# Shorter score bursts, 512-wide first products and a ScalarE-first order in a planned attention and two-MLP kernel

## The chip, the cores and the metric

The kernel runs on one core of a Trainium2 chip. The metric is device time in microseconds of one execution; the median of several executions is compared. Engines are named as the profile names them: PE is TensorE (PEld its weight loads), DVE VectorE, ACT ScalarE, POOL GpSimd, SP SyncE, which here issues nearly all DMAs.

## What is computed

```python
# attention, B=2, S=3008, D=256, d_qk=64
scores = matmul(z, z.T) / S              # symmetric: the queries are the keys
out    = u * matmul(maximum(scores, 0) ** 2, v)
x      = out.reshape(6016, 256)
# first MLP, d_ff = 2048
h = x @ w_in;  x = (h - tanh(h)) @ w_out
# second MLP, d_ff = 2048, its own weights and alpha
h = x @ w_in;  x = (maximum(h, 0) + alpha * minimum(h, 0)) @ w_out
```

Every factor is kept as a pair of rounded numbers, a high part and a low rest, and a product of two factors is three matmuls: high by high, low by high, high by low.

## The kernel before

**Who sets the order.** The kernel is written as a list of operations (`add`, L141 on) with what each reads and writes. PE's operations stand in a fixed order that `build` writes out; all others (ACT, DVE, DMAs on SP) are placed by a planner (`Plan.run`) that plays the program through with its own costs before a single instruction is recorded. It takes, whenever an engine is free, the ready operation with the earliest due time, a due time being worked out backward from the matmul that needs the result. An operation that either ACT or DVE could do stands in both lists, with a penalty on DVE. `turn` asks the engines in the order DVE, ACT, SP. The result is a fixed order of instructions on each engine; at run time each engine goes through its own in that order and waits on semaphores.

**Attention.** Queries come in 12 blocks of 512 (the last of each batch 448), keys in tiles of 128. For each block PE runs one "back" step for each key tile (`back`, 6 matmuls into two accumulator banks, weights from v). What a step needs are squared scores. Half of the scores follow from symmetry by a transpose and a way through DRAM (`flip`); the other half are computed in bursts of score tiles (`score_group`). In a burst two tiles at a time use the upper and the lower 64 rows of PE's array, 3 matmuls each, with one PSUM bank for each tile; a relu on ACT or DVE (L796, L798) empties the bank, then follow a square (L812, L814), a cast for the high part (L477, L478) and a subtraction for the low one (L820). There are 8 banks, of which the running block holds two. `GROUPS` and `MOST` give the sizes of the bursts of a block, `FIRST` the steps before which the bursts of the very first block stand; other bursts stand `LEADS` = 6 steps ahead of the first step that uses them.

**MLPs.** Tokens come in 6 supers of 1024 (the third and the sixth of 960, called narrow: halves of 480 columns). A unit is 2 of the 16 slices of d_ff for one super. All but the first super of each MLP use seven half-size products in place of eight (`stage`, `product_op`), with combinations of x and of the weights; the weights' combinations, called sums (`need_sums`, L665, L671), are made once on DVE, split, stored and loaded again. A unit's 21 forward matmuls alternate with the 24 backward ones (`back`) of units `LAG` = 28 steps earlier. The first MLP needs, for each slice, five passes of 1024 on ACT (L922) and some on DVE (L930, L933, L936); the second a leaky relu (L906, L908). The second MLP's x is the first one's result by way of DRAM: stored (L1092), loaded and split (`need_x`, L712, L477, L510). Its first product stands at least `X_STEPS` = 8 backward steps behind the step that finishes that super.

**The fill.** [...]

```python
if start and n < NB:
    nc.tensor.matmul(out=bank_tiles[at][:, n:NB], lhsT=lhsT, rhs=rhs[:, :NB - n], start=False, stop=True, ...)
```

Of the kernel before, what the change touches and what calls it, by code (L numbers as in the profile page):

```python
# [20 lines left out]
NB = 512  # L21
# [5 lines left out]
CHOOSE = 0.155  # L27
GROUPS, MOST = {(0, 0): (4, 4, 8, 8), (1, 0): (24,), (0, 1): (20,), (1, 1): (20,)}, 12
COMPUTED = frozenset()
LEADS = 6  # L30
FIRST = (0, 0, 3, 8)
NARROW = 2
# [7 lines left out]
W1_DUE, W2_DUE = (40.0, 250.0), (250.0, 450.0)  # L40
SUMS_DUE, SUMS_AHEAD = ((480.0, 550.0), (550.0, 600.0)), 60.0
SEVEN = {1: 1, 2: 1}
UNITS_AT = ((200, 11, 8),)
LAG, SHRINK, LAG_END, X_STEPS = 28, 64, 12, 8
KEEP_FREE, KEEP_SLACK = 0.5, 0.5
PART_AHEAD, X_AHEAD, SPLIT_AHEAD = 22.0, 30.0, 25.0

# [9 lines left out]
def pe_us(n):  # L57
    return n / 2400.0 + SLOT
# [67 lines left out]
class Plan:  # L126
# [71 lines left out]
    def run(self, cold=5.0, first=1.45):  # L198
# [8 lines left out]
        pe_at = 0  # L207
# [62 lines left out]
        def in_the_way(op, e, t):  # L270
# [10 lines left out]
            return False  # L281

        def turn(t):
            nonlocal pe_at
            for e in (DVE, ACT, SP):
                if busy[e] > t + 1e-9:
# [7 lines left out]
                while j < len(lst):  # L294
                    op = self.ops[lst[j][1]]
                    if op.start is not None:
                        del lst[j]
                        continue
                    if e in coming and in_the_way(op, e, t):
                        j += 1  # L300
                        continue
                    if allowed(op, t):
                        del lst[j]
                        start(op, e, t, op.engines[e] * (1.0 if e == SP else MARGIN))
                        break
                    j += 1
# [67 lines left out]
def attention_two_mlps_kernel(  # L374
# [380 lines left out]
    def score_group(group, lead):  # L755
        pairs = [group[e:e + 2] for e in range(0, len(group), 2)]
        for p, pair in enumerate(pairs):
# [18 lines left out]

            us = 3 * pe_us(max(blocks[i][2] for i, _ in pair)) * 1.02
            us += 0.23 * ((p == 0 and lead) + (p == len(pairs) - 1))
            add(("score", pair[0]), {PE: us}, emit, set(reads), keys, tail=0.21)
# [93 lines left out]
    def unit(kind, s, p):  # L873
# [68 lines left out]
        def product_op(name, ps, part, j, x, c0, first=False):  # L942
# [3 lines left out]
            def emit(_):  # L946
# [3 lines left out]
                for e, (ww, xx, cc) in enumerate(((wh, xh, c), (wl, xh, c), (wh, xl, cl))):  # L950
                    product(ps, m, ww, xx[:, cc:cc + m], first and e == 0, e == 2, skip_group_check=True)

            return add(("seven", kind, s, p, name), {PE: 3 * pe_us(m)}, emit, [w, h] if c0 is None else [w, h, l], [ps],
                       tail=0.21)
# [296 lines left out]
```

## Time and profile before

| | us |
|---|---|
| median of 3 runs | 1463.01 (1462.87 to 1463.58) |
| the profiled execution | 1461.6 |
| its span, first to last instruction | 1459.8 |
| PE busy | 1448.1 (99%) |
| DVE busy | 1335.9 (92%) |
| ACT busy | 1204.6 (83%) |

The profiled execution is one of its own and lies 1.4 us under the median. A matmul's row in the trace lasts from its start to its modelled end, longer than the spacing to the next start, so that rows overlap and PE can be busy in the page while it issues less than it could: the spacing of starts tells what a stretch costs. Idle time that stands in brackets behind a row of the timeline came right before that row, with what ended it.

### The profile page before, as it was taken

Reading aid. Unit: us, or ns where it says so; the run is one execution under the profiler, and the core shown is the slowest. Engines: PE = TensorE matmul, PEld = TensorE weight load, DVE = VectorE, ACT = ScalarE, POOL = GpSimd, SP = SyncE. Lnnn points to the kernel's source line nnn. Section 1 sums busy time; section 2 is a strip of 40 time slices with the busy share of each in tenths; the row PEclk is TensorE's granted clock in tenths of the full one; section 3 lists DMA queues with packets and bytes.
Section 4 is the critical chain, followed back from the end, with each engine's and each line's share of the span. In section 5 each row is a group of like instructions: output and inputs, shape, how many; then the busy total and the mean of one; then the engine's idle time right before and its main releaser. Section 6 shows DMA issues by size and latency. Waiting matters only on the chain.

```text
span 1459.8 us, 19079 instructions
## 1 busy us (share of the span) xinstructions
PE 1448.1 (99%) x6675; PEld 1198.3 (82%) x6675; DVE 1335.9 (92%) x1639; ACT 1204.6 (83%) x1620; POOL 0.2 (0%) x4
## 2 busy tenths in 40 slices
PE   9999999999999999999999999999999999999998
PEld 6787888787888888788888888888888888888887
DVE  9999988999999999998899999999999999999664
ACT  8967547677998989996999989997999989996332
POOL 0000000000000000000000000000000000000000
PEclk9999999999999999999999999999999999999999
DMA  7899885889788887733546354544555354636310
GB/s 260 247 283 285 296 289 183 231 276 284 219 273 259 279 269 266 266 119 123 162 162 194 124 187 146 202 154 154 186 181 180 122 175 143 233 118 226 120 58 28
DMA packets 203807, 290.61 MB, mean 199 GB/s; under 512 B 24640, under 2 KB 133824, under 8 KB 203712
## 3 DMA queue, kind: packets, MB, share of 16 engines
q1 hardware_dynamic: 203568, 289.28, 62.5%
q8 instruction: 53, 0.87, 0.2%
q14 instruction: 42, 0.34, 0.1%
q10 hardware_dynamic: 144, 0.12, 0.0%
HBM read 215.56 MB, written 73.79 MB: 198 GB/s over the span
## 4 chain that ended last, share of the span: by engine, by line
PE 94%; ACT 4%; DVE 1%; issue 0%; DMA 0%; SPq 0%; DVEq 0%; ACTq 0%
PE bank L469 94%; ACT sb L477 2%; ACT sb L922 1%; ACT sb L812 1%; ACT sb L796 1%; DVE sb L510 0%; DMA sb<-in_v 0%; DVE sb L908 0%; DVE sb L933 0%; DVE sb L814 0%; PE bank L471 0%; DVE sb L478 0%; ACT sb L906 0%; DVE sb L930 0%; DVE sb L665 0%
## 5 line engine op out<-in xcount | busy, mean ns | idle before, releaser
L469 PE MATMUL bank<-sb,sb 128*128 128x512 f32 (+3 forms) x6456 | 1429.2, 389 | 5.8 <-ACT sb L477 4.1
L469 PEld LDWEIGHTS bank<-sb,sb 128*128 128x128 f32 (+1 forms) x6456 | 1169.3, 188 | 246.0 <-issue 8.3
L922 ACT ACTIVATE sb<-sb 128x1024 f32<-128x1024 f32 (+1 forms) x480 | 478.8, 1041 | 8.2 <-DVE sb L478 4.4
L477 ACT CAST sb<-sb 128x1024 fp32r<-128x1024 f32 (+4 forms) x389 | 367.5, 992 | 29.3 <-DMA sb<-flip 16.0
L510 DVE TENSOR_TENSOR sb<-sb,sb 128x1024 fp32r<-128x1024 f32 (+2 forms) x276 | 300.5, 1106 | 6.2 <-ACT sb L477 5.2
L477 ACT COPY sb<-bank 128x512 f32<-128x512 f32 (+1 forms) x231 | 132.0, 579 | 53.5 <-PE bank L469 50.3
L906 ACT ACTIVATE sb<-bank 128x512 f32<-128x512 f32 (+1 forms) x152 | 89.4, 588 | 63.8 <-PE bank L469 59.8
L936 DVE COPY_PREDICATED sb<-sb,sb 128x1024 f32<-128x1024 int32 (+1 forms) x96 | 131.2, 1371 | 0.1
L908 DVE SCALAR_TENSOR_TENSOR sb<-sb,rest,bank 128x512 f32<-128x512 f32 (+1 forms) x152 | 110.9, 733 | 12.3 <-ACT sb L906 11.8
L933 DVE TENSOR_TENSOR sb<-sb,sb 128x1024 f32<-128x1024 f32 (+1 forms) x96 | 114.8, 1198 | 0.2 <-ACT sb L922 0.2
L930 DVE TENSOR_TENSOR sb<-sb,sb 128x1024 f32<-128x1024 f32 (+1 forms) x96 | 114.3, 1198 | 0.6 <-ACT sb L922 0.4
L796 ACT ACTIVATE sb<-bank 128x512 f32<-128x512 f32 (+1 forms) x153 | 77.3, 669 | 42.7 <-PE bank L469 42.5
L820 DVE TENSOR_TENSOR sb<-sb,sb 128x1024 fp32r<-128x1024 f32 (+2 forms) x88 | 100.8, 1161 | 2.1 <-ACT sb L477 1.9
L962 DVE TENSOR_TENSOR bank<-bank,sb 128x512 f32<-128x512 f32 (+1 forms) x80 | 54.8, 685 | 35.7 <-PE bank L469 33.7
L834 DVE STREAM_TRANSPOSE flip<-sb 128x512 f32<-128x512 f32 x120 | 76.3, 685 | 0.6 <-ACT sb L812 0.5
L812 ACT ACTIVATE sb<-sb 128x1024 f32<-128x1024 f32 (+2 forms) x68 | 72.4, 1160 | 0.0
L866 DVE TENSOR_TENSOR sb<-sb,sb 128x1024 fp32r<-128x1024 f32 (+1 forms) x60 | 70.3, 1175 | 0.9 <-ACT sb L477 0.7
L962 DVE TENSOR_TENSOR sb<-bank,sb 128x512 f32<-128x512 f32 (+1 forms) x80 | 54.0, 675 | 17.8 <-PE bank L469 17.7
L477 ACT COPY bank<-bank 128x512 f32<-128x512 f32 (+1 forms) x73 | 41.7, 571 | 18.5 <-PE bank L469 17.9
L593 ACT ACTIVATE sb<-sb 128x512 int32<-128x512 int32 x32 | 22.3, 697 | 34.8 <-DVE sb L591 34.8
L478 DVE COPY sb<-bank 128x512 f32<-128x512 f32 (+2 forms) x50 | 33.5, 671 | 18.3 <-PE bank L469 18.0
L478 DVE CAST sb<-sb 128x1024 fp32r<-128x1024 f32 (+3 forms) x51 | 31.2, 619 | 5.6 <-ACT sb L812 3.0
(35 smaller groups left out, 338.8 us busy)
## 6 DMA issues: line engine op xcount, KB each, us to landing
sb<-w SPq DMA_DIRECT2D x96, 512.0 KB, 4.7
sb<-wo SPq DMA_DIRECT2D x96, 512.0 KB, 4.7
sb<-w SPq DMA_DIRECT2D x80, 384.0 KB, 3.9
flip<-flip SPq DMA_DIRECT2D x100, 256.0 KB, 4.8
sb<-flip SPq DMA_DIRECT2D x40, 512.0 KB, 5.9
w<-sb SPq DMA_DIRECT2D x64, 256.0 KB, 3.9
sb<-flip SPq DMA_DIRECT2D x20, 448.0 KB, 6.4
sb<-in_moe_w_in SPq DMA_DIRECT2D x16, 512.0 KB, 6.0
```

What stands on the lines that cost most here:

```text
L469: nc.tensor.matmul(out=bank_tiles[at][:, :n], lhsT=lhsT, rhs=rhs, start=start, stop=stop, **how)
L477: return nc.scalar.copy(out=out, in_=in_)
L510: add(("low", l), {DVE: dve_us(n)}, lambda e: nc.vector.tensor_sub(out=r32(l)[:, o:o + n], in0=f32(src)[:, c0:c0 + n], in1=f32(h)[:, o:o + ...
L796: nc.scalar.activation(out=f32(a)[:, c0:c0 + n], in_=bank(ps)[:, :n], func=AF.Relu, scale=scale)
L820: add(("low", lp), {DVE: dve_us(w)}, lambda engine, c0=c0, w=w: nc.vector.tensor_sub(out=r32(l)[:, c0:c0 + w], in0=f32(a)[:, c0:c0 + w], i ...
L906: add(("relu2", part), {ACT: act_psum_us(m) if from_bank else act_us(m)}, lambda g: nc.scalar.activation(out=f32(f)[:, c0:c0 + m], in_=src ...
L908: add(("leak", part), {DVE: 0.06 + dve_us(m)}, lambda g: nc.vector.scalar_tensor_tensor(out=f32(f)[:, c0:c0 + m], in0=f32(f)[:, c0:c0 + m] ...
L922: add((name, to), {ACT: act_us(n)}, lambda e: nc.scalar.activation(out=f32(to)[:, :n], in_=f32(inp)[:, :n], func=func, **how), reads, [to] ...
L930: add(("subtract", ts), {DVE: us}, lambda e: nc.vector.tensor_sub(out=f32(ts)[:, :n], in0=f32(f)[:, :n], in1=f32(ts)[:, :n]), parts, [ts], ...
L933: add(("series", f), {DVE: us}, lambda e: nc.vector.tensor_mul(out=f32(f)[:, :n], in0=f32(f)[:, :n], in1=f32(gs)[:, :n]), [gs, ts], [*part ...
L936: add(("choose", ts), {DVE: CHOOSE + us}, lambda e: nc.vector.copy_predicated(out=f32(ts)[:, :n], mask=f32(gs)[:, :n].bitcast(I32), data=f ...
L962: add(("add", to), {DVE: dve_us(m)}, lambda e: nc.vector.tensor_add(out=out(), in0=bank(t)[:, :m], in1=f32(fifth)[:, :m]), reads, [to], **how)
```

## The change

Six things change, most of them numbers that the planner reads.

- Bursts hold at most six tiles (`MOST` 12 to 6, `GROUPS` cut to the first block, whose bursts are 4, 4, 6, 6, 4; `FIRST` gets a fifth place). There were 17 groups (two of them side by side), now there are 33.
- The first of the three matmuls of a first product (`product_op` with `first`) is 512 wide also in a narrow unit, reading 32 columns beyond its half; so `product` writes no fill there. The second and third stay 480 wide.
- `left_to_act`: DVE doesn't take an operation that ACT could finish 15 us ahead of its due time behind all that is due earlier on it; and ACT is asked first.
- The sums' due times: first MLP 500 and 545 us in place of 480 and 550, second MLP 640 and 680 in place of 550 and 600.
- `X_STEPS` 8 to 12: the second MLP's first product of a super stands at least 12 backward steps behind the end of the first one's.
- `LAG` 28 to 26, and the costs that the planner gives to score bursts and to wide first products.

```diff
-GROUPS, MOST = {(0, 0): (4, 4, 8, 8), (1, 0): (24,), (0, 1): (20,), (1, 1): (20,)}, 12
+GROUPS, MOST = {(0, 0): (4, 4, 6)}, 6
-FIRST = (0, 0, 3, 8)
+FIRST = (0, 0, 3, 8, 13)
-SUMS_DUE, SUMS_AHEAD = ((480.0, 550.0), (550.0, 600.0)), 60.0
+SUMS_DUE, SUMS_AHEAD = ((500.0, 545.0), (640.0, 680.0)), 60.0
-LAG, SHRINK, LAG_END, X_STEPS = 28, 64, 12, 8
+LAG, SHRINK, LAG_END, X_STEPS = 26, 64, 12, 12
+ACT_SLACK = 15.0
...
+        def left_to_act(op, t):
+
+            if op.engines.get(ACT) is None:
+                return False
+            at = max(busy[ACT], t)
+            for due, index in ready[ACT]:
+                if due > op.due:
+                    break
+                other = self.ops[index]
+                if other is not op and other.start is None:
+                    at += other.engines[ACT] * MARGIN
+            late = max(busy[PE] - self.pe[pe_at].nominal, 0.0) if pe_at < len(self.pe) else 0.0
+            return at <= op.due + late - ACT_SLACK
+
...
-            for e in (DVE, ACT, SP):
+            for e in (ACT, DVE, SP):
...
-                    if e in coming and in_the_way(op, e, t):
+                    if e in coming and in_the_way(op, e, t) or e == DVE and left_to_act(op, t):
...
-            us = 3 * pe_us(max(blocks[i][2] for i, _ in pair)) * 1.02
-            us += 0.23 * ((p == 0 and lead) + (p == len(pairs) - 1))
+            us = 3 * pe_us(max(blocks[i][2] for i, _ in pair)) * 1.03
+            us += 0.1 * ((p == 0 and lead) + (p == len(pairs) - 1))
...
-                    product(ps, m, ww, xx[:, cc:cc + m], first and e == 0, e == 2, skip_group_check=True)
+                    n = NB if first and e == 0 else m
+                    product(ps, n, ww, xx[:, cc:cc + n], first and e == 0, e == 2, skip_group_check=True)
```

What this does to the order of instructions is shown at three places.

PE, the first narrow unit of the first MLP (its third super): the first two first products, in banks 77 and 80, with weights sb_5856. Before:

```order
L469 MATMUL bank_77<-sb_6056,sb_5856 128x480
L471 MATMUL bank_77<-sb_6056,sb_5856 128x32
L469 MATMUL bank_77<-sb_6056,sb_5856 128x480 x2
L469 MATMUL bank_80<-sb_6038,sb_5856 128x480
L471 MATMUL bank_80<-sb_6038,sb_5856 128x32
L469 MATMUL bank_80<-sb_6038,sb_5856 128x480
L469 MATMUL bank_80<-sb_6082,sb_5856 128x480
```

The same unit after, with banks 76 and 77 and weights sb_5960:

```order
L484 MATMUL bank_76<-sb_6049,sb_5960 128x512
L484 MATMUL bank_76<-sb_6049,sb_5960 128x480 x2
L484 MATMUL bank_77<-sb_6115,sb_5960 128x512
L484 MATMUL bank_77<-sb_6115,sb_5960 128x480
L484 MATMUL bank_77<-sb_6137,sb_5960 128x480
```

The two fills are gone and the first of each three is 512 wide; nothing else in the unit changes its shape.

ACT, the first work of the kernel: relus (out of a bank) of the first eight score tiles and what stands ahead of them; sb_149, sb_159 and sb_145 receive z and v. Before:

```order
L477 CAST sb_170<-sb_149 128x512
L796 ACTIVATE sb_192<-bank_74 128x512
L796 ACTIVATE sb_192<-bank_75 128x512
L796 ACTIVATE sb_206<-bank_76 128x512
L796 ACTIVATE sb_206<-bank_77 128x512
L477 CAST sb_218<-sb_192 128x512
L796 ACTIVATE sb_223<-bank_78 128x512
L796 ACTIVATE sb_223<-bank_79 128x512
```

After (the third cast, of sb_181, reads v):

```order
L492 CAST sb_165<-sb_145 128x512
L492 CAST sb_170<-sb_149 128x512
L492 CAST sb_181<-sb_149 128x512
L492 CAST sb_191<-sb_159 128x512
L811 ACTIVATE sb_194<-bank_74 128x512
L811 ACTIVATE sb_205<-bank_76 128x512
L827 ACTIVATE sb_194<-sb_194 128x512
L811 ACTIVATE sb_205<-bank_77 128x512
L811 ACTIVATE sb_222<-bank_78 128x512
L811 ACTIVATE sb_222<-bank_79 128x512
```

Three casts moved from DVE to ACT and stand ahead of its first relu; one of the relus (bank 75) went to DVE.

DVE, ahead of the second MLP's first product: sb_5503 and sb_5514 are its x, whose casts are on ACT before (into sb_5564 and sb_5572); L671 and the 512-wide L510 belong to the sums. Before:

```order
L671 TENSOR_TENSOR sb_3640<-sb_3640,sb_3637 128x512
L510 TENSOR_TENSOR sb_5516<-sb_5317,sb_5499 128x1024
L510 TENSOR_TENSOR sb_5519<-sb_4807,sb_5465 128x512
L510 TENSOR_TENSOR sb_5534<-sb_3637,sb_5501 128x512
L510 TENSOR_TENSOR sb_5534<-sb_3640,sb_5519 128x512
L930 TENSOR_TENSOR sb_5416<-sb_5116,sb_5416 128x1024
L930 TENSOR_TENSOR sb_5536<-sb_5136,sb_5536 128x1024
L933 TENSOR_TENSOR sb_5116<-sb_5116,sb_5405 128x1024
L933 TENSOR_TENSOR sb_5136<-sb_5136,sb_5522 128x1024
L930 TENSOR_TENSOR sb_5560<-sb_5202,sb_5560 128x1024
L510 TENSOR_TENSOR sb_5570<-sb_5503,sb_5564 128x1024
L510 TENSOR_TENSOR sb_5575<-sb_5514,sb_5572 128x1024
```

After, x is sb_5461 and sb_5470, and the first cast is DVE's own:

```order
L686 TENSOR_TENSOR sb_5314<-sb_5334,sb_5314 128x512
L525 TENSOR_TENSOR sb_5491<-sb_5328,sb_5478 128x1024
L951 COPY_PREDICATED sb_5425<-sb_5409,sb_5143 128x1024
L945 TENSOR_TENSOR sb_5502<-sb_5202,sb_5502 128x1024
L680 TENSOR_TENSOR sb_5353<-sb_5353,sb_5314 128x512
L493 CAST sb_5525<-sb_5461 128x1024
L525 TENSOR_TENSOR sb_5534<-sb_5425,sb_5516 128x1024
L525 TENSOR_TENSOR sb_5538<-sb_5461,sb_5525 128x1024
L948 TENSOR_TENSOR sb_5202<-sb_5202,sb_5468 128x1024
L525 TENSOR_TENSOR sb_5558<-sb_5470,sb_5546 128x1024
```

The splits of the sums (512-wide L510, L525 after) no longer stand ahead of the split of x, and x's first cast has moved to DVE.

## Rows read from the trace of the kernel before

**Rows 1.** The page: busy time by engine, and the chain of waits.
```profile
PE 1448.1 (99%) x6675; PEld 1198.3 (82%) x6675; DVE 1335.9 (92%) x1639; ACT 1204.6 (83%) x1620; POOL 0.2 (0%) x4
PE 94%; ACT 4%; DVE 1%; issue 0%; DMA 0%; SPq 0%; DVEq 0%; ACTq 0%
```

**Rows 2.** Windows, four bursts and all eleven: stretch, length, PE busy (matmuls), clock, DMA.
```profile
85.04:90.05 5.01, 5.01 (x37) 1.00 0.99 271
114.28:115.89 1.61, 1.61 (x13) 1.00 1.14 341
162.33:165.38 3.05, 3.05 (x26) 1.00 1.07 374
...
sum 57.87, PE 57.63; mean PE 5.24
```

**Rows 3.** Timeline of PE at a four-tile burst: start, length, work, count.
```profile
113.97 0.39 PE L469 MATMUL bank<-sb,sb 128*128 128x512 f32 x1
114.28 1.68 PE L469 MATMUL bank<-sb 64*128 64x512 f32 x12
115.89 0.95 PE L469 MATMUL bank<-sb,sb 128*128 128x512 f32 x3
```

**Rows 4.** Timeline of PE: narrow unit, plain stretches; and the group of fills.
```profile
685.47 0.18 PE L471 MATMUL bank<-sb,sb 128*128 128x32 f32 x1
685.49 0.90 PE L469 MATMUL bank<-sb,sb 128*128 128x480 f32 x3
686.23 0.18 PE L471 MATMUL bank<-sb,sb 128*128 128x32 f32 x1
...
609.77 20.56 PE L469 MATMUL bank<-sb,sb 128*128 128x512 f32 x90
1408.07 10.68 PE L469 MATMUL bank<-sb,sb 128*128 128x480 f32 x48
L471 PE MATMUL bank<-sb,sb 128*128 128x32 f32 x80 | 14.2, 178 | 0.0
```

**Rows 5.** Timelines of PE, SP, ACT near 600 us; windows by PE, PEld, DVE, ACT.
```profile
593.78 4.69 PE L469 MATMUL bank<-sb,sb 128*128 128x512 f32 x20
600.36 0.49 PE L469 MATMUL bank<-sb,sb 128*128 128x512 f32 x1 [1.89 <-ACT sb L477]
602.25 4.03 PE L469 MATMUL bank<-sb,sb 128*128 128x512 f32 x10 [1.40 <-ACT sb L477]
590.22 0.45 SPq L712 DMA_DIRECT2D sb<-yd  x1
593.57 5.80 ACT L922 ACTIVATE sb<-sb 128x1024 f32<-128x1024 f32 x6
598.50:602.20 3.70, 0.49 (x1) 0.19 (x1) 3.70 (x4) 3.70 (x5) 0.00 (x0) 0.97 1.10 365
602.20:605.70 3.50, 3.44 (x9) 2.72 (x10) 3.50 (x4) 3.50 (x5) 0.00 (x0) 0.54 1.04 388
```

**Rows 6.** The first 45 us: timelines, a window, the chain, a group.
```profile
8.45 30.95 PE L469 MATMUL bank<-sb,sb 128*128 128x512 f32 x148 [0.79 <-ACT sb L477]
40.76 4.41 PE L469 MATMUL bank<-sb,sb 128*128 128x512 f32 x26 [1.36 <-DVE sb L820]
23.00:43.00 20.00, 18.58 (x88) 13.32 (x88) 19.80 (x31) 20.00 (x29) 0.00 (x0) 1.00 0.88 230
1.64 3.99 DMA sb<-in_v
5.59 2.07 ACT L796 ACTIVATE sb<-bank 128x512 f32<-128x512 f32 x4 [0.94 <-PE bank L469]
L477 ACT CAST sb<-sb 128x512 fp32r<-128x512 f32 x54 | 33.8, 655 | 2.3 <-DMA sb<-in_zT 1.8 <-DMA sb<-in_v 0.2 <-DVE sb L814 0.2
```

**Rows 7.** Windows of a narrow and a wide stretch of the MLPs.
```profile
685.00:765.00 80.00, 80.00 (x371) 67.68 (x369) 66.77 (x76) 71.37 (x95) 0.00 (x0) 1.00 0.49 155
765.00:847.00 82.00, 82.00 (x371) 69.04 (x370) 78.02 (x92) 76.04 (x107) 0.00 (x0) 1.00 0.55 174
```

More of the change, by code (lines that the diff above doesn't have):

```diff
@@ L950, in emit @@
                 for e, (ww, xx, cc) in enumerate(((wh, xh, c), (wl, xh, c), (wh, xl, cl))):
-                    product(ps, m, ww, xx[:, cc:cc + m], first and e == 0, e == 2, skip_group_check=True)
-            return add(("seven", kind, s, p, name), {PE: 3 * pe_us(m)}, emit, [w, h] if c0 is None else [w, h, l], [ps],
+                    n = NB if first and e == 0 else m
+                    product(ps, n, ww, xx[:, cc:cc + n], first and e == 0, e == 2, skip_group_check=True)
+            return add(("seven", kind, s, p, name), {PE: 3 * pe_us(m) + first * (NB - m) / 2400.0}, emit, [w, h] if c0 is None else [w, h, l], [ps],
                        tail=0.21)
```

## The prediction

> **What bounds the kernel now.** I read the page first: TensorE is busy for 1448.1 of 1459.8 us, and the chain of waits runs through it for 94% of the span [rows 1]. So the whole gain to be had is time in which TensorE issues nothing, issues slower than it can, or issues matmuls that need not exist. A busy share of 99% hides most of that, because a matmul's row lasts some 0.39 us while the next one starts 0.227 us after it: 90 matmuls of 512 columns in 20.56 us make (20.56 - 0.39) / 89 = 0.2266 us each, and 48 of 480 columns in 10.68 us make (10.68 - 0.38) / 47 = 0.219 us [rows 4]. I therefore went through the timeline of TensorE and compared starts with these two spacings. Four places stand out: the bursts of score products [rows 2, 3], the narrow units of both MLPs [rows 4], a standstill near 600 us [rows 5] and the first 45 us [rows 6]. Elsewhere starts follow each other at the spacing.
>
> **Narrow units: the fill goes.** Before, a first product of 480 columns is followed by a 32-column matmul with the same weights that fills the bank. In the timeline one such fill starts at 685.47 and the next at 686.23: 0.76 us for three products of 480 and one fill. The three would take 3 x 0.219 = 0.657 us; the fill itself takes 0.02 (the next matmul starts at 685.49), and the other 0.08 us come right behind it: the three matmuls that start at 685.49 take 0.74 us to the next fill instead of 0.657 [rows 4]. I read this as a weight load that the short fill is too short to cover. After, the three are one of 512 and two of 480: 0.2266 + 0.438 = 0.665 us, so 0.095 less. There are 80 fills [rows 4]; 2 MLPs x 2 narrow supers x 2 halves x 2 banks = 16 belong to the backward products and stay, 2 x 2 x 8 units x 2 first products = 64 go. 64 x 0.095 = **6.1 us**, all of it on TensorE's path; between 5.0 and 6.5. What comes next there is ScalarE, busy for 71.4 of 80 us in a narrow stretch, and VectorE, 66.8 [rows 7]; taking 1.5 us out of each such stretch leaves both below it.
>
> [...]
>
> **The standstill near 600 us.** Twenty matmuls start at 593.78, so the next is due at 593.78 + 20 x 0.2266 = 598.31; it starts at 600.36, and the one behind it, due at 600.59, at 602.25; both waited for a cast on ScalarE [rows 5]. That is 2.05 + 1.66 us. Then the granted clock stands at 0.54 (the lower level, 1.2 GHz, for nearly the whole stretch) from 602.2 to 605.7, after the engine had been busy for 0.49 of 3.70 us: 9 matmuls in 3.5 us instead of 2.04 [rows 5]. Together **5.2 us**. The product that waits is the second MLP's first use of its x: x was stored, loaded back (the first load is issued at 590.22) and then split; ScalarE had six passes of another unit ahead of the cast, and neither it nor VectorE was idle in those 3.7 us [rows 5]. The change acts on three sides of this: the first use comes 12 instead of 8 backward steps behind the last one of the first MLP's super, 4 x 6 x 0.2266 = 5.4 us later; the sums of the second MLP's weights are due 80 us or more later, so their passes no longer stand on VectorE right ahead of x's split; and the first of the two casts is VectorE's. 5.4 us of new room against 3.7 us of waiting, so I take the whole 5.2; between nothing and 5.6. The next such hand-overs have tens of microseconds of room in the order, since another whole block stands between store and use.
>
> **Bursts of six.** Eight banks less two accumulators leave six. A burst of four tiles takes 1.61 us from its first score product to the next full one, one of eight 3.05, so a tile costs 0.36 and a burst 0.17; one of twelve takes 5.01 instead of 0.17 + 12 x 0.36 = 4.49 [rows 2], since from the seventh tile on a product waits for a bank that ScalarE empties. Outside these windows a change of the array's tiling costs 0.31 - 0.227 = 0.08 us going in and 0.95 - 0.39 - 2 x 0.227 = 0.11 us behind the way out [rows 3]. The eleven bursts past the first block hold 136 tiles and take 57.87 us together [rows 2]. After, these tiles are 26 bursts: 20 of six at 2.33, 2 of four at 1.61, 4 of two at 0.89, in sum 53.4. That saves 4.5, and 15 more bursts at 0.19 take back 2.9: **1.6 us** gained. If every six waits for banks half as much as that twelve did, it is 20 x 0.25 = 5.0 us worse, a loss of 3.4; if none pays more than its tiles, up to 2.2 gained.
>
> **The first 45 us.** TensorE stood idle for 0.79 us before 8.45 and for 1.36 before 40.76, the latter behind a split of the last score tiles, with ScalarE busy for 20.00 and VectorE for 19.80 of the 20 us before 43 [rows 6]. After, the third and fourth burst hold 6 and 4 tiles in place of 8, and a burst of the next block (six tiles, 2.3 us) stands ahead of that pair, which gives the two engines the time that was missing: 1.5 us gained there. The row from 8.45 holds 148 matmuls in 30.95 us; 100 full ones at 0.2266 and two bursts of eight at 3.05 + 0.19 make 29.3 with the last one's tail, so 1.65 us went into smaller waits, of which I take 0.6. Against it stand one more burst, 0.17 + 0.19 = 0.36 us, and the planner's new first turn for ScalarE: it now has four casts ahead of the first relu, the third of them of v, which lands at 1.64 + 3.99 = 5.63 us. Before, the first relu started at 5.59; after, two casts of 0.655 us come first, the second overlapping the first's end, so it starts up to 1.2 us later [rows 6]. VectorE takes one relu, so I take 0.7 of it. In sum **1.0 us** gained, between 2.5 gained and 2.0 lost.
>
> **What is moved at no cost.** ScalarE first: counted in the order, 24 casts go from VectorE to ScalarE with 6 relus and 5 squares, and 19 bank copies the other way. Both engines have room in the wide units (76.04 and 78.02 of 82 us [rows 7]), and TensorE's work hides them; where that room is gone, a cast would show with its own length. I take nothing, between 0.5 gained and 3 lost. The shorter lag of the backward products (26 steps for 28) takes 2 x 1.36 us from a lead of 28 x 1.36 = 38 us: nothing.
>
> **The sum.** 6.1 + 5.2 + 1.6 + 1.0 = 13.9 us off the profiled execution's own 1461.6 us (span 1459.8 and 1.8 around it): 1447.7. The median of the runs stands 1.4 above that execution, so 1463.0 - 13.9 = **1449.1 us**, 0.95% less.
>
> **Rivals.** (A) The standstill stays or moves: the store, load and split of x still end late, or the sums collide with another unit near 660 us, and the clock falls again. For it: VectorE and ScalarE are saturated there [rows 5]. Against it: 5.4 us of new room. 1449.1 + 5.2 = 1454.3 us. (B) The banks are not free when a six begins, since ScalarE has a pass or a cast in hand: +5.0, 1454.1 us. For it: relus of VectorE became fewer, casts on ScalarE more. Against it: most bursts stand 30 or more full matmuls (6.8 us) apart and six relus, four of which take 2.07 us [rows 6], need about 3. The Trainium skill, "TensorEngine Tiling (Array Packing)", section "PSUM Bottleneck", says to use both engines for emptying banks; the change does less of that, and by that rule this rival is what happens. (C) The 0.08 us behind a fill belong to something else, such as the change of bank, and stay: by 64 x 0.08 = 5.1 us less gain, 1454.2 us. Against it: the wide units, which change banks as well, show no such gap. (D) Slower than before: ScalarE becomes the bound in the MLPs. In the wide stretch it is busy for 76.04 of 82 us [rows 7]; the moves add some 18 us of passes to it in the whole kernel, while TensorE's time shrinks. It decides only from the point where ScalarE needs more than TensorE's 82 us for eight units; at 83.5 us, 1.5 over, the eleven blocks of eight lose 17 us and the time is 1466. That takes 7.5 us more passes in every block, some 80 in all, where 18 are added.
>
> **How the numbers follow.** My forecast with its own bounds has 0.64, A 0.13, B 0.10, C 0.06, D 0.03, a better one (1444 to 1446) 0.04. The lower end, 1445.5, takes in the best values of three terms; the upper, 1455.5, takes in A, B and C one at a time with a microsecond to spare. Within 0.2% (2.9 us, about what a measurement of this kernel can tell from no change) is reached only if A, B and C come together: 0.03. Faster 0.94, slower 0.03.
>
> **What would show it.** In the profile after: 16 matmuls of 32 columns in place of 80 and a unit of a narrow super that takes 10.1 instead of 10.28 us; no idle time of TensorE and a granted clock of 1.00 where the second MLP begins; bursts of six at 2.3 to 2.4 us without a bank's wait; an idle time before the first backward product of 1.0 to 2.0 us in place of 0.79 and none near 41 us; ScalarE busier, VectorE less busy. It is wrong if bursts of six cost 2.6 us or more, or if a new stretch of the MLPs shows a granted clock below 1.00.

## The result and the profile after

The changed kernel takes **1446.76 us** in the median of four runs (1446.37 to 1448.04), the kernel before 1462.94 us in runs beside it: a ratio of 0.989, with a 95% interval of 0.987 to 0.991. The prediction was 1449.1 us, with a range from 1445.5 to 1455.5. The profiled execution of after takes 1446.52 us, its span 1444.7 us; of before they were 1461.6 and 1459.8. So 15.1 us have to be found between the two traces; the medians stand 16.2 apart, since before's profiled execution was 1.3 us under its median and after's 0.2. That last microsecond lies between runs, and no trace shows it.

The page of after, with the busy time by engine, the chain of waits and the costliest group, answers [rows 1]:

```profile
PE 1438.0 (100%) x6611; PEld 1186.0 (82%) x6611; DVE 1326.8 (92%) x1623; ACT 1223.2 (85%) x1636; POOL 0.2 (0%) x4
...
PE 98%; ACT 1%; DMA 0%; DVE 0%; SPq 0%; issue 0%
...
L484 PE MATMUL bank<-sb,sb 128*128 128x512 f32 (+3 forms) x6456 | 1419.3, 388 | 1.0 <-DVE sb L493 0.7
```

TensorE makes 64 matmuls fewer (6611 for 6675), the chain runs through it for 98% instead of 94%, and its whole idle time in the costliest group is 1.0 us. ScalarE is busier by 18.6 us and VectorE less by 9.1, as the moves of work say. The rest is read place by place.

**The bursts** [rows 2]. Windows from a burst's first score product to the next full one: a burst of six, of two, of four, and the sum of all 26 past the first block.

```profile
67.49:69.80 2.31, 2.31 (x20) 1.61 (x19) 2.31 (x5) 1.30 (x3) 0.00 (x0) 1.00 0.96 313
79.52:80.42 0.90, 0.90 (x7) 0.48 (x6) 0.90 (x1) 0.00 (x0) 0.00 (x0) 1.00 0.88 293
...
112.41:114.02 1.61, 1.61 (x14) 1.06 (x13) 1.61 (x4) 0.60 (x2) 0.00 (x0) 1.00 1.32 301
...
sum 52.90, PE 52.90 PEld 36.36 DVE 46.56 ACT 35.02 POOL 0.00; mean PE 2.03 PEld 1.40 DVE 1.79 ACT 1.35 POOL 0.00
```

All twenty bursts of six take 2.29 to 2.31 us, whatever else ScalarE and VectorE have in hand there: none waits for a bank. The sum was 57.87 before and is 52.90.

**The narrow units** [rows 4]. The group of fills in after, and then the window of one narrow unit of the first MLP (from the first product of one to the first product of the next):

```profile
L486 PE MATMUL bank<-sb,sb 128*128 128x32 f32 x16 | 2.8, 178 | 0.0
```

```profile
690.48:700.56 10.08, 10.08 (x47) 8.45 (x45) 8.91 (x11) 9.89 (x13) 0.00 (x0) 1.00 0.58 170
```

The same unit in the kernel before:

```profile
695.75:706.03 10.28, 10.28 (x49) 8.67 (x48) 8.48 (x10) 9.73 (x14) 0.00 (x0) 1.00 0.52 155
```

Two matmuls fewer, and 0.20 us shorter, 0.10 for each fill.

**Near 600 us** [rows 5]. First the window of 22 us in the kernel before, then in after:

```profile
590.00:612.00 22.00, 18.71 (x75) 14.80 (x74) 22.00 (x24) 22.00 (x28) 0.00 (x0) 0.92 0.97 322
```

```profile
590.00:612.00 22.00, 22.00 (x99) 18.22 (x98) 21.94 (x24) 21.82 (x28) 0.00 (x0) 1.00 0.84 288
```

Before, 75 matmuls ran in these 22 us and the granted clock was 0.92 in the mean; after, 99 ran without any idle time, at a clock of 1.00. 24 matmuls at 0.2266 are 5.4 us. ScalarE and VectorE are as saturated as before; the casts are only no longer late.

**The first 45 us** [rows 6]. The timeline of ScalarE and TensorE in after:

```profile
5.89 1.25 ACT L492 CAST sb<-sb 128x512 fp32r<-128x512 f32 x2 [1.22 <-DMA sb<-in_v]
7.06 1.08 ACT L811 ACTIVATE sb<-bank 128x512 f32<-128x512 f32 x2
...
9.43 3.03 PE L484 MATMUL bank<-sb,sb 128*128 128x512 f32 x12 [0.70 <-DVE sb L493]
```

A window of 8 us around the place where TensorE stood idle for 1.36 us before:

```profile
36.00:44.00 8.00, 8.00 (x41) 6.04 (x41) 8.00 (x13) 8.00 (x13) 0.00 (x0) 1.00 0.89 240
```

ScalarE's casts wait for v, so its first relu starts at 7.06 instead of 5.59 and the first backward product at 9.43 instead of 8.45. Against that the idle time near 40 us is gone: TensorE is busy for all of the 8 us, where the same window of before has 6.64. Right ahead of the next block's first burst TensorE has started the same work in both kernels, 115 full products (7 of them the bf16 ones that it begins with) and 72 score products: at 42.79 us before and at 42.28 us after, so the start is 0.5 us shorter.

### The profile page after: what moved, and what is told of

Read it like the earlier page. It is cut to its first block, busy times and chain, and to the rows that moved or that the text cites. A ratio compares the mean times of both kernels' runs of the same rounds, so it can differ in the third digit from the quotient of the medians.

```text
span 1444.7 us, 18872 instructions
## 1 busy us (share of the span) xinstructions
PE 1438.0 (100%) x6611; PEld 1186.0 (82%) x6611; DVE 1326.8 (92%) x1623; ACT 1223.2 (85%) x1636; POOL 0.2 (0%) x4
## 4 chain that ended last, share of the span: by engine, by line
PE 98%; ACT 1%; DMA 0%; DVE 0%; SPq 0%; issue 0%
PE bank L484 98%; ACT sb L811 0%; DMA sb<-in_v 0%; ACT sb L492 0%; DVE sb L835 0%; ACT sb L827 0%; SPq L542 0%; PE bank L486 0%; DVE sb L493 0%
## 5 line engine op out<-in xcount | busy, mean ns | idle before, releaser
L492 ACT CAST sb<-sb 128x1024 fp32r<-128x1024 f32 (+3 forms) x413 | 384.6, 973 | 17.3 <-DVE sb L923 12.1
L525 DVE TENSOR_TENSOR sb<-sb,sb 128x1024 fp32r<-128x1024 f32 (+2 forms) x276 | 300.6, 1106 | 11.4 <-ACT sb L492 11.1
L492 ACT COPY sb<-bank 128x512 f32<-128x512 f32 (+1 forms) x222 | 126.5, 578 | 52.4 <-PE bank L484 48.6
L921 ACT ACTIVATE sb<-bank 128x512 f32<-128x512 f32 (+1 forms) x152 | 89.7, 590 | 53.1 <-PE bank L484 50.9
L811 ACT ACTIVATE sb<-bank 128x512 f32<-128x512 f32 (+1 forms) x159 | 81.6, 618 | 58.9 <-PE bank L484 58.9
L827 ACT ACTIVATE sb<-sb 128x1024 f32<-128x1024 f32 (+2 forms) x73 | 75.4, 1074 | 0.5 <-DVE sb L813 0.4
L493 DVE COPY sb<-bank 128x512 f32<-128x512 f32 (+2 forms) x59 | 39.7, 673 | 20.4 <-PE bank L484 20.0
L492 ACT COPY bank<-bank 128x512 f32<-128x512 f32 (+1 forms) x63 | 36.2, 575 | 13.0 <-PE bank L484 12.5
L923 DVE SCALAR_TENSOR_TENSOR sb<-sb,rest,sb 128x512 f32<-128x512 f32 (+1 forms) x40 | 28.7, 736 | 0.0
```

What stands on the lines that cost most here:

```text
L492: return nc.scalar.copy(out=out, in_=in_)
L525: add(("low", l), {DVE: dve_us(n)}, lambda e: nc.vector.tensor_sub(out=r32(l)[:, o:o + n], in0=f32(src)[:, c0:c0 + n], in1=f32(h)[:, o:o + ...
L811: nc.scalar.activation(out=f32(a)[:, c0:c0 + n], in_=bank(ps)[:, :n], func=AF.Relu, scale=scale)
L921: add(("relu2", part), {ACT: act_psum_us(m) if from_bank else act_us(m)}, lambda g: nc.scalar.activation(out=f32(f)[:, c0:c0 + m], in_=src ...
L923: add(("leak", part), {DVE: 0.06 + dve_us(m)}, lambda g: nc.vector.scalar_tensor_tensor(out=f32(f)[:, c0:c0 + m], in0=f32(f)[:, c0:c0 + m] ...
```

## The experiments

The theory was the prediction's sum, term by term: fills, standstill, bursts, and moves that cost nothing. The rival for every term was that the gain belongs to something else: to a change of bank, to the sums' due times, to the new order on ScalarE.

### The fills alone, and fills of other widths

Three kernels take up the fill, each from the kernel before. The first makes the first product 512 wide, which takes 64 fills away and leaves the order of all other work as it was:

```diff
+                    n = NB if first and e == 0 else m
-                    product(ps, m, ww, xx[:, cc:cc + m], first and e == 0, e == 2, skip_group_check=True)
+                    product(ps, n, ww, xx[:, cc:cc + n], first and e == 0, e == 2, skip_group_check=True)
```

> The kernel before with one edit: the first matmul of a first product is 512 wide in narrow units too, so that 64 of the 80 fills go; the planner's costs stay, so every other instruction stands where it stood. Theory (a fill costs its own 0.02 us and 0.08 us of a weight load that it is too short to cover): 64 x 0.095 = 6.1 us less, about 1456.9. Rival (only the fill's own issue floor counts, the 0.08 us belong to something else): 64 x 0.02 = 1.2 us less, about 1461.7.

Measured: 1456.04 us (1455.07 to 1456.45), beside 1462.71 of before, a ratio of 0.9953 (0.9936 to 0.9969): **6.7 us** less, 0.104 for each fill. In its trace, counted product by product against before, the part from the first narrow unit on is 6.5 us shorter: 6.1 at the 64 places themselves, 0.095 each, and 0.4 in the last 50 us, where the other products of 480 columns stand a little closer (0.216 apart, 0.219 before). The rival, 1.2 us less, is out. The other two keep all fills and make them wider, so that they overlap part of what was written:

```diff
-            nc.tensor.matmul(out=bank_tiles[at][:, n:NB], lhsT=lhsT, rhs=rhs[:, :NB - n], ...
+            nc.tensor.matmul(out=bank_tiles[at][:, NB - 192:NB], lhsT=lhsT, rhs=rhs[:, :192], ...
```

> The kernel before with every fill made 192 columns wide in place of 32 or 64 (it adds into real columns of the first products, so the result of the MLPs changes; the number of instructions and their order don't). Theory (what costs is the next weight load, some 0.11 us that runs beside the fill): a fill of 192 columns lasts about 0.09 us and only takes the place of the gap, so the time stays within 1 us of before, and the start of the next product behind a fill comes at the same distance. Rival (the gap of 0.08 us comes on top of whatever the fill lasts): 84 fills of full height x 160 / 2400 us = 5.6 us more, about 1468.5.

Measured: 1463.96 us (1.25 more), ratio 1.0007 (0.9998 to 1.0016). With 416 columns in place of 192:

> As the kernel with fills of 192 columns, with 416 columns (the result of the MLPs changes in the same way). Theory: a fill of 416 columns lasts about 0.187 us, longer than the weight load, so no gap is left behind it: 0.187 - 0.109 = 0.078 us more for each of 84, 6.5 us more than before, about 1469.5. Rival (the gap stays on top): 84 x 384 / 2400 = 13.4 us more, about 1476.3.

Measured: 1470.88 us (8.2 more), ratio 1.0056 (1.0041 to 1.0071). The timeline of TensorE with fills of 192 at the place that [rows 4] shows:

```profile
688.08 0.25 PE L471 MATMUL bank<-sb,sb 128*128 128x192 f32 x1
688.17 0.83 PE L469 MATMUL bank<-sb,sb 128*128 128x480 f32 x3
688.84 0.25 PE L471 MATMUL bank<-sb,sb 128*128 128x192 f32 x1
```

From fill to fill it is 0.76 us, just as with 32 columns, though the fill now holds TensorE for 0.09 us instead of 0.02: the three products behind it take 0.67 us and no longer 0.74. So the 0.08 us is not a price of changing the bank; the product right behind a fill even goes into the same bank. It is time in which TensorE has to wait after a matmul too short to cover it, and a wider fill fills it with columns. With 416 columns the fill takes 0.19 us and everything beyond the gap is lost: in the trace 6.6 us of the 8.2 come from the first narrow unit on, where 6.5 were foretold for all. Some 0.8 us of what 192 columns cost, and 1.5 of what 416 do, come instead in the two blocks of 448 columns (the last experiment comes back to them). That it is the next weight load that the short fill fails to cover was the prediction's reading and fits all three; the runs show the gap's length and that it is hidden under a longer matmul, not what happens in it.

### The second MLP's first use alone

The kernel before, with `X_STEPS` 12 in place of 8:

```diff
-LAG, SHRINK, LAG_END, X_STEPS = 28, 64, 12, 8
+LAG, SHRINK, LAG_END, X_STEPS = 28, 64, 12, 12
```

> The kernel before with X_STEPS 12 alone: the second MLP's first use of x comes four backward steps, 5.4 us, later. Theory (room between the store of x and its first use is what was missing): idle time of TensorE there under 0.5 us, no fall of the clock, 4.5 to 5.2 us less, 1457.8 to 1458.5. Rival (the sums of the second MLP hold VectorE and ScalarE, and x is split late however long it has been there): a wait of over 2 us stays, less than 2.5 us gained.

Measured: 1461.01 us, 1.9 less than the 1462.91 beside it, ratio 0.9987 (0.9978 to 0.9997). The place itself did what was foretold: a window of 590 to 612 us has 98 matmuls at a clock of 1.00. But the timeline of TensorE has four new waits that neither before nor after shows:

```profile
663.30 1.20 PE L469 MATMUL bank<-sb,sb 128*128 128x512 f32 x4 [0.35 <-ACT sb L477]
665.18 17.30 PE L469 MATMUL bank<-sb,sb 128*128 128x512 f32 x75 [0.68 <-DVE sb L510]
732.78 2.52 PE L469 MATMUL bank<-sb,sb 128*128 128x480 f32 x10 [1.13 <-DVE sb L962]
1079.64 94.37 PE L469 MATMUL bank<-sb,sb 128*128 128x512 f32 x415 [0.94 <-DVE sb L962]
```

In starts against the plain spacing the four cost 3.9 us. One number moved, the planner made another order of everything behind it, and that order has late splits (L477, L510) and late additions (L962, the sums of half-size products) elsewhere.

### The sums' due times alone, and both together

```diff
-SUMS_DUE, SUMS_AHEAD = ((480.0, 550.0), (550.0, 600.0)), 60.0
+SUMS_DUE, SUMS_AHEAD = ((500.0, 545.0), (640.0, 680.0)), 60.0
```

> The kernel before with the sums' due times of the changed kernel alone. Theory (the standstill near 600 us is too short a way from the store of x to its first use, with saturated engines on top): the wait for x shrinks but stays over 1 us with the clock falling behind it, 0 to 3 us less. Rival (the sums' passes alone held up the split of x): the standstill goes, 5.2 us less, about 1457.8.

Measured: 1463.86 us, 1.1 more, ratio 1.0008 (0.9999 to 1.0018). The standstill stays, in three pieces:

```profile
599.87 0.50 PE L469 MATMUL bank<-sb,sb 128*128 128x512 f32 x1 [1.01 <-DVE sb L478]
601.60 1.57 PE L469 MATMUL bank<-sb,sb 128*128 128x512 f32 x4 [1.23 <-ACT sb L477]
603.88 8.35 PE L469 MATMUL bank<-sb,sb 128*128 128x512 f32 x25 [0.71 <-DVE sb L510]
```

VectorE has the first cast now, and no split of a sum stands ahead of it, yet the product still waits: later due times for the sums do not by themselves bring x in time. They move only a part of the sums' work, since four passes of 0.7 us that form sums (L665, L671) still run on VectorE between 591 and 601 us, one of them between x's first cast and its split. What a place with no sums at all would give was not tried. The interval of this ratio includes no change at all. With the later first use as well:

> The kernel before with two parts: the second MLP's first use of its x 12 steps behind in place of 8, and the sums' new due times. Alone they gave 1.9 us less and 1.0 us more. If the waits that the later first use brought (near 663, 733 and 1080 us) came from sums of the second MLP standing on VectorE, the new due times take them away: 1457.7 us, the whole standstill of 5.2 us gained. My theory is that they came from VectorE taking work that ScalarE had room for, which neither part changes: some of them stay, 1459.5 to 1462 us.

Measured: 1460.39 us, 2.3 less than the 1462.65 beside it, ratio 0.9985 (0.9976 to 0.9994), within what the theory gave and 2.7 us above the rival. The theory's sign failed, though: none of the waits at 663, 733 and 1080 us stayed, and two others came. Around the first of them, VectorE and TensorE:

```profile
901.39 1.23 DVE L933 TENSOR_TENSOR sb<-sb,sb 128x1024 f32<-128x1024 f32 x1
...
902.53 0.68 DVE L962 TENSOR_TENSOR sb<-bank,sb 128x512 f32<-128x512 f32 x1
...
903.27 0.98 PE L469 MATMUL bank<-sb,sb 128*128 128x512 f32 x3 [1.31 <-DVE sb L962]
```

The addition that TensorE needs takes 0.68 us; a pass of 1.23 us that nobody waits for yet stands ahead of it on VectorE. That is what such a wait is made of. The theory named VectorE taking work that ScalarE had room for; this pass is VectorE's own (only it does L933), so of that mechanism the run shows only that VectorE is late, not that ScalarE's work made it so.

### The same number taken back in the kernel after

```diff
-LAG, SHRINK, LAG_END, X_STEPS = 26, 64, 12, 12
+LAG, SHRINK, LAG_END, X_STEPS = 26, 64, 12, 8
```

> The changed kernel with X_STEPS back at 8. Theory: the standstill returns at least in part, since the way from store to first use is 5.4 us shorter again and nothing but the sums has left: 2 to 5 us more, 1449 to 1452, with an idle time of TensorE where the second MLP begins. Rival (the sums were the cause): the same time as the changed kernel, within 0.5 us.

Measured: 1450.60 us, 3.8 more than after, ratio to before 0.992 (0.9904 to 0.9937). The timeline of TensorE shows where:

```profile
596.60 1.20 PE L484 MATMUL bank<-sb,sb 128*128 128x512 f32 x4 [0.17 <-ACT sb L492]
598.28 150.83 PE L484 MATMUL bank<-sb,sb 128*128 128x512 f32 x668 [0.48 <-DVE sb L525]
1299.83 1.14 PE L484 MATMUL bank<-sb,sb 128*128 128x480 f32 x4 [0.71 <-ACT sb L492]
1302.15 81.28 PE L484 MATMUL bank<-sb,sb 128*128 128x480 f32 x360 [1.19 <-DVE sb L525]
```

Near 600 us only 1.2 us are lost, and the clock does not fall; 2.4 us go at 1300 us, where products 480 columns wide wait for a cast and a split (1024 columns each) that are in time in after. So with the rest of the change the early use is cheaper than it was, and most of the price of taking the number back is another place of the new order.

### Bursts of other lengths in the kernel after

The old lists, with bursts of up to 24 tiles (24 and 20 in three blocks, twelve at most elsewhere):

```diff
-GROUPS, MOST = {(0, 0): (4, 4, 6)}, 6
+GROUPS, MOST = {(0, 0): (4, 4, 8, 8), (1, 0): (24,), (0, 1): (20,), (1, 1): (20,)}, 12
-FIRST = (0, 0, 3, 8, 13)
+FIRST = (0, 0, 3, 8)
```

> The changed kernel with the groups of before (up to 24 tiles in a burst, 17 groups). Theory: long bursts wait for banks again, 4.5 to 5 us, and save 16 changes of tiling at 0.19 plus 0.17 us, with the wait near 41 us back: 2 to 4 us more in sum, 1448.5 to 1451. Rival (what a change of tiling costs outweighs the waits): the same or up to 1.5 us less.

Measured: 1452.81 us, 6.05 more than after, ratio to before 0.9932 (0.9917 to 0.9947). The spans stand 5.5 apart (1450.2 and 1444.7), and 2.5 of that is the same wait at 1300 us, which leaves some 3 us for the bursts, the upper half of what was expected:

```profile
1301.46 1.14 PE L484 MATMUL bank<-sb,sb 128*128 128x480 f32 x4 [0.75 <-ACT sb L492]
1303.84 81.28 PE L484 MATMUL bank<-sb,sb 128*128 128x480 f32 x360 [1.24 <-DVE sb L525]
```

Bursts of at most four, eight more of them:

```diff
-GROUPS, MOST = {(0, 0): (4, 4, 6)}, 6
+GROUPS, MOST = {(0, 0): (4, 4, 6)}, 4
```

> The changed kernel with MOST 4: bursts of four behind the first block, 8 bursts more, none of which can run out of banks. Theory (a burst costs 0.17 us in its window and 0.19 outside it, and bursts of six wait for nothing already): 8 x 0.36 = 2.9 us more, about 1449.7. Rival (bursts of six still wait for banks): the shorter ones save that, and the time is the same or less.

Measured: 1449.87 us (1449.80 to 1450.22), 3.1 more than after, 0.39 for each burst added; ratio to before 0.9912 (0.9897 to 0.9927). Six is the best of the three lengths: more wait for banks, fewer pay 0.39 us more often.

### ScalarE first: taken from after, and given to before

The part that the prediction took at nothing, taken out of the kernel after:

```diff
-            for e in (ACT, DVE, SP):
+            for e in (DVE, ACT, SP):
...
-                    if e in coming and in_the_way(op, e, t) or e == DVE and left_to_act(op, t):
+                    if e in coming and in_the_way(op, e, t):
```

> The kernel after, with the planner's turn for ScalarE taken back: VectorE is asked first again and takes what it can get. My theory, formed from the run of the later first use of x alone: what keeps 1.0 to 1.4 us waits of TensorE away at several places of the second MLP is that ScalarE takes all it can, so that VectorE is free when a sum or a return of a product is due. Without it such waits come back behind VectorE, two to three of them, and the time is 1449 to 1451 us (after is 1446.8). The rival, the prediction's own step (what is moved is hidden and costs nothing): 1446 to 1447.5 us, no new wait. Around the first 10 us both expect up to 1 us less, since the first relu need not stand behind four casts.

Measured: 1448.45 us (1448.23 to 1448.71), 1.7 more than after, ratio to before 0.9901 (0.9887 to 0.9914), a little under what the theory gave and above the rival. The start is better, as both expected: the first backward product begins at 8.83 instead of 9.43, and at the end of the attention this kernel is 0.66 us ahead of after. Then it loses 2.4 us, 1.8 of them at 1300 us:

```profile
8.83 19.16 PE L484 MATMUL bank<-sb,sb 128*128 128x512 f32 x96 [0.55 <-ACT sb L492]
...
1298.01 1.13 PE L484 MATMUL bank<-sb,sb 128*128 128x480 f32 x4 [0.24 <-ACT sb L492]
1300.14 81.25 PE L484 MATMUL bank<-sb,sb 128*128 128x480 f32 x360 [1.00 <-DVE sb L525]
```

The waits behind additions that the theory foretold did not come; the one that came is the place that two other variants also lost. And the same part given to the kernel before, alone (with the function `left_to_act` and the order ACT, DVE, SP):

```diff
-            for e in (DVE, ACT, SP):
+            for e in (ACT, DVE, SP):
...
-                    if e in coming and in_the_way(op, e, t):
+                    if e in coming and in_the_way(op, e, t) or e == DVE and left_to_act(op, t):
```

> The kernel before with one part alone: ScalarE is asked first and is left what it can make in time. The prediction's step said 0.5 gained to 3 lost, taken as nothing: 1462.4 to 1466, and 1462.9 as its value. My theory now: by itself it gives little, since the standstill near 600 us is set by the first use of x and stays or shrinks by the one cast that moves: 1461 to 1463 us. The rival, that this order is worth several microseconds by itself in the second MLP: 1458 to 1460 us, with waits gone near 1142 to 1158 us and near 40 us.

Measured: **1469.39 us** (1468.51 to 1470.20), 6.7 more, ratio 1.0044 (1.0031 to 1.0056). Both the theory and the rival missed, and the prediction's own bound (3 lost) too. The timeline of TensorE, and then two windows at the standstill:

```profile
603.39 0.80 PE L484 MATMUL bank<-sb,sb 128*128 128x512 f32 x1 [3.38 <-ACT sb L492]
739.41 2.54 PE L484 MATMUL bank<-sb,sb 128*128 128x480 f32 x10 [1.12 <-DVE sb L977]
750.21 2.52 PE L484 MATMUL bank<-sb,sb 128*128 128x480 f32 x10 [0.19 <-DVE sb L977]
761.77 2.53 PE L484 MATMUL bank<-sb,sb 128*128 128x480 f32 x10 [0.99 <-DVE sb L977]
1166.18 15.92 PE L484 MATMUL bank<-sb,sb 128*128 128x512 f32 x69 [0.67 <-DVE sb L525]
```

```profile
600.00:603.40 3.40, 0.01 (x2) 0.01 (x1) 3.07 (x4) 3.40 (x5) 0.00 (x0) 0.98 1.07 413
603.40:608.00 4.60, 4.41 (x9) 2.70 (x10) 4.14 (x4) 4.60 (x6) 0.00 (x0) 0.50 1.03 420
```

More work went to ScalarE where x's casts stood in its queue already: the wait grew to 3.4 us in one piece, and the clock then stayed at its lower level (1.2 GHz, 0.50) for 6.8 us where before had 3.4. Counted product by product against before, the standstill costs 2.0 us more, the additions (L977, which is L962 of before) and the split at 1166 us, late on VectorE, another 4.2, and what comes ahead of the standstill 1.5.

### Twelve fills fewer

A version meant to beat both kernels: the kernel after, with the first product of a backward step 512 wide too where its half begins at column 0, so that 8 fills of 32 columns and 4 of 64 go.

```diff
-                product(accs[d], n, r32(w)[:, c:c + P], r32(x)[:, c0:c0 + n], first and e == 0, last and e == len(todo) - 1)
+                m = NB if first and e == 0 and not c0 else n
+                product(accs[d], m, r32(w)[:, c:c + P], r32(x)[:, c0:c0 + m], first and e == 0, last and e == len(todo) - 1)
```

> The kernel after, in which the first product of a backward step is 512 wide too where its half begins at column 0, so that 12 of the 16 fills that were left go. My theory: a fill costs 0.10 us as the 64 fills did (6.7 us for 64), so 12 x 0.10 = 1.2 us less, 1445.6 us. The rival: these fills stand two in a row at a place with four other products of the step around them and their gaps are part of the change of banks, 0.02 us each, 1446.5 us.

Measured: 1446.56 us (1446.40 to 1447.10) against 1446.76 (1446.37 to 1448.04) of after: no difference that these runs can tell. The profiled execution shows why the question stays open. ScalarE's cast of v and TensorE's first backward product:

```profile
6.51 1.31 ACT L492 CAST sb<-sb 128x512 fp32r<-128x512 f32 x2 [1.70 <-DMA sb<-in_v]
...
10.05 3.04 PE L484 MATMUL bank<-sb,sb 128*128 128x512 f32 x12 [2.07 <-DVE sb L493]
```

v landed 0.6 us later in this execution, the slowest of the four, in the same order of instructions at the start; that is no part of the median. Counted product by product against after, the trace tells where the gain went. The theory holds at the fills: each pair of narrow fills gives back 0.17 to 0.19 us, 0.7 in all, and the four fills of 64 columns 0.35. But in the two blocks that are 448 columns wide the products behind the widened one now start 0.2064 us apart in the mean and no longer 0.2035, and that takes 1.0 us back. The same slower step stands in the two kernels with wider fills (0.2071 and 0.2064) and in none of the others (0.2034 to 0.2041). What it comes from no run here shows.

## Why the prediction was right, and where its steps were off

**The fills: right.** Forecast 6.1, between 5.0 and 6.5; measured 6.7 between the medians, where the interval allows 4.5 to 9.4. In that kernel's trace the 64 places give 6.1, the 0.095 us each of the forecast, and the closer steps at the end another 0.4, which the forecast did not have. The Trainium skill ("TensorE: Matmul & The Clock Gate", section "Back-to-back issue gap") gives a matmul of 1 to 64 columns an issue floor of about 25 ns, and the fill's own 0.02 us agrees. The same section says that in a stream of weight loads and matmuls both set the spacing and that its formula comes out too low for short matmuls; it gives no such spacing for 32 columns, and the 0.08 us behind the fill are this case's own figure. Rival C falls with them.

**The standstill: right in sum, wrong in its reasons.** The whole 5.2 us came back, in the trace of after and at that place also with the later use alone. But the three sides that I named don't carry it alike. The later use alone removes the wait; all the rest without it leaves 1.2 us of it; the sums' due times alone leave it standing (with the first cast on VectorE, but with a part of the sums still there), and ScalarE first alone makes it worse. I wrote that the next hand-overs have tens of microseconds of room and let the term stand there. What the runs show in place of that: the planner answers to every number with a new order, and that order can have late splits and additions hundreds of microseconds on. The later use alone won 5.2 us at its place and gave some 4 back elsewhere.

**The bursts: right.** Forecast 53.4 us for all 26 and 2.9 for fifteen more entries and exits, 1.6 gained; measured 52.90, a gain of 4.97. From the end of the start to the end of the attention TensorE wins 1.7 us in all, so the fifteen took some 3.2. Six tiles for six free banks never wait, so rival B falls, and with it, for this kernel, what the Trainium skill ("TensorEngine Tiling (Array Packing)", section "PSUM Bottleneck") would have made of the time: six relus fewer are on VectorE, and no burst became longer.

**The start: right in its parts, half in its sum.** Forecast 1.0, measured 0.5. The idle time near 40 us went, 1.5 us as foretold, but the first backward product came 1.0 us later, where 0.7 was taken. One sign foretold for it, an idle time of 1.0 to 2.0 us ahead of that product, does not stand in this trace (0.70), because the first burst ran slower in this execution and took part of the delay on itself (below). The kernel with bursts of four, whose first instructions are the same, has it:

```profile
6.48 1.56 PE L484 MATMUL bank<-sb,sb 64*128 64x512 f32 x12
9.39 3.05 PE L484 MATMUL bank<-sb,sb 128*128 128x512 f32 x12 [1.35 <-DVE sb L493]
```

So the backward product waits for v's cast and split, and begins at 9.4 us in both, whether the burst ahead of it was fast or slow.

**What is moved at no cost: the step that was wrong in its reason.** In the sum the value nothing did little harm, since together with the other parts ScalarE first gains 1.7 us. But it was argued from busy shares, "both engines have room", and the bound of 3 us was not one: given to the kernel before, the same part cost 6.7. A share of 76 in 82 us does not say what stands ahead of the one cast that TensorE waits for. Some 2.0 us of that cost stand at the late hand-over: while x's casts were late, more work on ScalarE made them later, at the lower clock as well. The rest are late additions and a late split elsewhere, and the start. That the same work fits once x has 12 steps of room is read from after, which differs in other parts too, and was not tried apart.

**The sum.** Counted in the traces it is 6.5 + 5.2 + 1.7 + 0.5 = 13.9, the very sum that was forecast; that it meets it so closely is partly luck, since the start was taken 0.5 too large and the 0.4 beside the fills were not foreseen. The profiled executions differ by 15.1: another 0.5 us are smaller waits near 1159 us that also went, and 0.7 stand at no single place. These 1.2, and 1.1 more in how the medians stand to the traces, make the 2.3 us by which the time came out below. The parts measured alone on the kernel before do not add up to it: fills 6.7 and later use 1.9 gained, sums 1.1 and ScalarE first 6.7 lost, in sum 0.8 gained for 16.2 together (bursts and lag were not tried alone). Each but the fills is a new plan, with the new waits that their traces show. Rival D, ScalarE as the bound in the wide stretches, did not come: TensorE was never idle there, with ScalarE at 75.97 and VectorE at 77.50 of 80 us:

```profile
757.00:837.00 80.00, 80.00 (x362) 67.55 (x361) 77.50 (x91) 75.97 (x105) 0.00 (x0) 1.00 0.54 169
```

**What stays open.** Why the place near 1300 us is in time in after and late in three variants that each change something else (the first use, the bursts, the order of engines): the runs show that it is late, not which instruction ahead of it decides. Why the products of the 448-wide blocks step 0.2064 us apart in some kernels and 0.2035 in others is open too. Nor was the lag of 26 tried apart, nor ScalarE first together with the later use alone.

## What to carry to other kernels

Look at the spacing of starts, not at busy time: a matmul of 32 columns that fills a bank cost 0.10 us, five times its own 0.02 us, and the cure was to make the matmul ahead of it as wide as the bank. Look at the spacing behind such a cure as well: in the 448-wide blocks of the last experiment it took back what the fills gave. Where a planner makes the order, a part tried alone measures that part plus a new plan: see whether the place meant got better and list the waits that appeared elsewhere before calling the part useless or good. And a burst that empties through banks should hold as many tiles as there are banks free: here six were better than four by 3.1 us and better than up to 24 by some 3.

## What was not expected of the hardware

A fill of 192 columns costs next to nothing more than one of 32 (1.25 us for 92 of them, with an interval that takes in zero), since its columns run in a gap that is there anyway. VectorE's cast of 1024 columns takes less than ScalarE's, 0.69 against 1.07 us in the mean of the groups in after:

```profile
L492 ACT CAST sb<-sb 128x1024 fp32r<-128x1024 f32 x249 | 257.0, 1068 | 5.4 <-DVE sb L923 4.9 <-DVE sb L739 0.3
...
L493 DVE CAST sb<-sb 128x1024 fp32r<-128x1024 f32 x17 | 11.7, 693 | 1.8 <-ACT sb L827 1.7
```

And in the first microseconds the same work runs at different speeds in different executions: the window from 4.50 to 7.00 us has 13 matmuls in after, shown first, and 21 in before.

```profile
4.50:7.00 2.50, 2.50 (x13) 2.04 (x14) 1.36 (x3) 1.27 (x3) 0.00 (x0) 1.00 1.00 349
```

```profile
4.50:7.00 2.50, 2.50 (x21) 2.03 (x22) 2.09 (x5) 1.56 (x4) 0.00 (x0) 1.00 0.93 335
```

In after the score products of the first burst, which run two side by side, start 0.425 us apart from one couple to the next up to about 7 us, in later bursts 0.23. That is the spacing of 512 columns at the lower of the two levels (512 / 1.2 GHz = 0.427 us). The clock of 1.00 in both windows does not speak against it: the record of the granted clock has its first entry, full clock, at 7.02 us in after and at 4.68 in before, and a window counts what lies ahead of that entry as 1.00. In all fourteen traces that entry comes between 4.67 and 7.29 us, and the couples stand 0.23 us apart behind it and 0.42 to 0.43 ahead of it, wherever a whole step past the first lies there. So the kernel begins at the lower level, after had it 2.3 us longer than before in these two executions, and an early window's 1.00 must be checked by the spacing. Why it rises at another time in each execution no run here tells.
